# Convolutions of four blocks in one TensorE visit instead of two

## The chip, the cores and the metric

One NeuronCore of one Trainium2 chip. The metric is the device time of the whole program in microseconds (us). A run is called slow when it is over 1.5% above the fastest of its kernel. The granted TensorE clock, the share of full speed that the chip lets TensorE run at, is given where it matters.

## The reference, cut to what matters

A depthwise causal convolution of width 7 (weights by softmax, one set for each of 8 heads of 24 channels) over `x[8, 4160, 192]`, then a feed-forward layer with a three-way maximum:

```python
y = conv7(x)                                          # (33280, 192)
h = maximum(maximum(y @ w1, y @ w2), y @ w3)          # (33280, 768)
out = h @ w_out                                       # (33280, 192)
```

The kernel uses max(a, b, c) = c + max(max(a-c, 0), b-c): "layer 1" computes the two differences, "layer 2" adds them up with w_out, and a product of w3 and w_out is applied to y directly.

## The kernel before

The tokens are cut into 65 blocks of 512. TensorE does three things: layer 1 (`l1`, six groups a block, 64-row tiles, one bank `p` and one bank `q` a group), layer 2 (`st2`, six portions a block, 64-row tiles, results `po` in banks `w`), and the convolution of a later block (`conv`, 32-column tiles, two banks). A bank is here one tile of 128 x 512 fp32 in the memory that takes the results of matmuls; the kernel allocates eight (two `p`, two `q`, four `w`). An evacuation copies a result out of its bank. A conv is a product with a band matrix, per chunk of about 103 tokens and per head:

```python
def conv(t, pools=((psw, "w"), (psw, "w"))):
    G = [pool.tile([P, NBLK], FP32, tag=tag, ...) for i, (pool, tag) in enumerate(pools)]
    for (q, b, row_lo, rlen, lo, hi, cc) in chunks_of[t]:        # 5 chunks
        for i in range(2):
            for g in range(4):
                ...
                nc.tensor.matmul(G[i][32 * g:32 * g + 32, lo:hi],
                                 lhsT=x16[0:rlen, cb:cb + 32], rhs=band[0:rlen, h, cc:cc + hi - lo],
                                 start=True, stop=True, tile_position=(0, 32 * g))
...
for t in range(2, NB):                                           # cut
    l1(t, 0)
    us = convs_at.get(t, (t + 3, t + 4) if t % 2 == 0 else ())
    for n, u in enumerate(us):
        conv(u, PQ if n else ((psw, "w"), (psw, "w")))
    for u in us:
        evac(u, 0)                                               # ScalarE
    for u in us[::-1]:
        evac(u, 1, nc.vector.tensor_copy)                        # VectorE
    ...                                                          # repacks, loads, casts
    st2(t - 1, 0, NJ)
    for j in range(1, NJ):
        l1(t, j)
        st2(t - 1, j, NJ)
```

So a conv is 40 matmuls with a weight load each, and every second block TensorE makes a visit of two convs. The result of a conv goes through `ys` (four slots), six repacking DMAs and a doubling DMA before layer 1 of that block reads it.

The softmax here doesn't subtract the row's maximum and nothing guards it: scores larger than these inputs give would overflow.

## Time and profile before

| | before |
|---|---|
| time | 480.37 us (479.93 to 480.54, 3 runs) |
| span of the profiled run, granted clock | 478.4 us, 0.999 |
| TensorE busy | 97% |
| a block without a visit, with a visit of two | 6.36, 7.59 us |
| four blocks | 27.90 us |

The blocks' times are the distances between the first layer-1 matmuls of blocks that follow each other. From block 6 to 62 the pattern repeats within 0.1 us. The lines themselves stand in the prediction.

### The profile page before, as it was taken

Reading aid. Unit: us, or ns where it says so; the run is one execution under the profiler, and the core shown is the slowest. Engines: PE = TensorE matmul, PEld = TensorE weight load, DVE = VectorE, ACT = ScalarE, POOL = GpSimd, SP = SyncE. Lnnn points to the kernel's source line nnn. Section 1 sums busy time; section 2 is a strip of 40 time slices with the busy share of each in tenths; the row PEclk is TensorE's granted clock in tenths of the full one; section 3 lists DMA queues with packets and bytes.
Section 4 is the critical chain, followed back from the end, with each engine's and each line's share of the span. In section 5 each row is a group of like instructions: output and inputs, shape, how many; then the busy total and the mean of one; then the engine's idle time right before and its main releaser. Section 6 shows DMA issues by size and latency. Waiting matters only on the chain.

```text
span 478.4 us, 21790 instructions
## 1 busy us (share of the span) xinstructions
PE 466.1 (97%) x9008; PEld 390.2 (82%) x9008; DVE 368.2 (77%) x612; ACT 323.6 (68%) x602; POOL 213.6 (45%) x346
## 2 busy tenths in 40 slices
PE   7799999999999999999999999999999999999996
PEld 3377888888888888888888888888888888888995
DVE  6776877877787787778778777877877787787774
ACT  4666667667666766766676676667667666766664
POOL 3645534543453454345345434534535453454200
PEclk9999999999999999999999999999999999999999
DMA  8786766666756676675576667666666766674323
GB/s 193 170 195 188 202 186 181 173 175 172 205 155 169 170 196 171 177 201 158 158 206 169 177 171 206 166 170 187 169 155 188 206 166 168 176 182 122 98 67 100
DMA packets 68576, 81.86 MB, mean 171 GB/s; under 512 B 9422, under 2 KB 57486, under 8 KB 68478
## 3 DMA queue, kind: packets, MB, share of 16 engines
q1 hardware_dynamic: 55310, 49.51, 42.2%
q0 software_dynamic: 13008, 30.88, 20.9%
q8 instruction: 70, 1.15, 1.1%
q14 instruction: 28, 0.23, 0.1%
q10 hardware_dynamic: 160, 0.10, 0.1%
HBM read 30.31 MB, written 25.56 MB: 117 GB/s over the span
## 4 chain that ended last, share of the span: by engine, by line
PE 94%; DVE 2%; DMA 2%; ACT 1%; issue 0%; ACTq 0%; SPq 0%
PE lp L365 31%; PE po L409 30%; PE lq L365 26%; PE G L295 7%; DMA yd<-ys 1%; DMA yd<-yd 1%; DVE h L370 0%; DVE yd L330 0%; PE D L314 0%; PE idle L211 0%; ACT L225 0%; DVE line L228 0%; ACT r L369 0%; PE band_cols L232 0%; DVE wd L250 0%
## 5 line engine op out<-in xcount | busy, mean ns | idle before, releaser
L370 DVE TENSOR_TENSOR h<-r,lq 128x512 f16<-128x512 f16 x390 | 267.1, 685 | 100.8 <-ACT r L369 100.5
L369 ACT ACTIVATE r<-lp 128x512 f16<-128x512 f32 x390 | 232.9, 597 | 140.5 <-PE lp L365 92.8
L365 PE MATMUL lp<-yd,wd 64*128 64x512 f16 x1170 | 315.7, 376 | 2.2 <-DVE wd L250 1.6
L365 PE MATMUL lq<-yd,wd 64*128 64x512 f16 x1170 | 314.3, 375 | 2.7 <-DVE h L370 1.8
L409 PE MATMUL po<-wo,h 64*128 64x192 f16 x3120 | 230.7, 243 | 0.0
L409 PEld LDWEIGHTS <-h 64*128 64x128 f16 x3120 | 186.3, 94 | 25.8
L365 PEld LDWEIGHTS <-wd 64*128 64x128 f16 x2340 | 163.6, 93 | 28.2 <-issue 4.4
L435 POOL DMA_DIRECT2D out_dram<-o x63 | 49.9, 793 | 235.0 <-DVE o L419 227.1
L348 POOL DMA_DIRECT2D yd<-ys x186 | 94.0, 509 | 4.3 <-ACT ys L335 1.7
L409 PE MATMUL po<-m,yd 64*128 64x192 f16 x780 | 86.9, 243 | 0.0
L419 DVE TENSOR_TENSOR o<-a,po 128x384 f32<-128x384 f32 (+1 forms) x132 | 71.4, 542 | 0.6 <-ACT a L418 0.6
L418 ACT COPY a<-po 128x384 f32<-128x384 f32 (+1 forms) x132 | 61.7, 468 | 1.4 <-PE po L409 1.4
L149 POOL CAST x<-xf 112x960 f16<-112x960 f32 x61 | 60.6, 995 | 4.5 <-DMA xf<-in_x_dram 4.5
L409 PEld LDWEIGHTS <-yd 64*128 64x128 f16 x780 | 54.7, 94 | 8.3
L335 DVE CAST ys<-G 128x512 f16<-128x512 f32 x62 | 39.8, 683 | 0.0
L295 PEld LDWEIGHTS <-x 112*32 112x32 f16 x2440 | 29.0, 96 | 13.3 <-issue 13.2
L335 ACT CAST ys<-G 128x512 f16<-128x512 f32 x62 | 33.5, 588 | 1.8 <-PE G L295 0.4
L295 PE MATMUL G<-band,x 112*32 112x103 f16 (+1 forms) x2440 | 33.8, 209 | 0.0
L166 POOL CAST xz<-xf 112x240 f16<-112x240 f32 (+2 forms) x12 | 3.8, 360 | 7.7 <-DMA xf<-in_x_dram 7.7
L211 PE MATMUL idle<-idle 128*128 128x512 f16 x10 | 4.6, 628 | 1.2 <-DVE idle L206 1.2
L314 PEld LDWEIGHTS <-xz 112*32 112x32 f16 x180 | 3.6, 111 | 1.4 <-issue 1.4
L330 DVE COPY yd<-yd 64x512 f16<-64x512 f16 x6 | 2.7, 452 | 1.9 <-ACT yd L320 1.2
(48 smaller groups left out, 44.7 us busy)
## 6 DMA issues: line engine op xcount, KB each, us to landing
out_dram<-o POOLq DMA_DIRECT2D x63, 384.0 KB, 4.1
xf<-in_x_dram SPq DMA_DIRECT2D x57, 420.0 KB, 4.5
yd<-yd SPq DMA_DIRECT2D x62, 192.0 KB, 3.3
yd<-ys SPq DMA_DIRECT2D x62, 48.0 KB, 3.8
yd<-ys POOLq DMA_DIRECT2D x62, 48.0 KB, 3.5
xf<-in_x_dram SPq DMA_DIRECT2D x8, 252.0 KB, 3.5
yd<-ys SPq DMA_DIRECT2D x62, 32.0 KB, 3.3
yd<-ys POOLq DMA_DIRECT2D x62, 32.0 KB, 3.5
```

What stands on the lines that cost most here:

```text
L149: nc.gpsimd.tensor_copy(out=v[0:rl, q0:q1, :], in_=xf[0:rl, q0:q1, :])
L211: nc.tensor.matmul(ps[:], lhsT=idle[:, 0:P], rhs=idle[:], start=True, stop=True)
L295: nc.tensor.matmul(G[i][32 * g:32 * g + 32, lo:hi], lhsT=x16[0:rlen, cb:cb + 32], rhs=band[0:rlen, h, cc:cc + hi - lo], start=True, stop=T ...
L335: copy(out=slots[t][:, i, :], in_=convs[t][i][:])
L348: (nc.sync, nc.gpsimd)[n % 2].dma_start(out=yd[r0:r0 + rows, c, :], in_=slots[t][s0:s0 + rows, half, :])
L365: nc.tensor.matmul(ps[i][:, 0:N], lhsT=wd[row, c, P * j:P * (j + 1)], rhs=y[row, c, 0:N], start=(c == 0), stop=(c == NC - 1))
L369: nc.scalar.activation(out=r[:, 0:N], in_=ps[0][:, 0:N], func=AF.Relu)
L370: nc.vector.tensor_max(out=hs[t][:, j, 0:N], in0=r[:, 0:N], in1=ps[1][:, 0:N])
L409: nc.tensor.matmul(ps[b0, i][:, s % 2, :], lhsT=a, rhs=b, start=first, stop=last)
L418: nc.scalar.copy(out=a[:, ss, :], in_=ps[s0, 0][:, ss, :])
L419: nc.vector.tensor_add(out=outs[t][:, s0:s + 1, :], in0=a[:, ss, :], in1=ps[s0, 1][:, ss, :])
L435: qs[i].dma_start(out=bass.AP(tensor=out.tensor, offset=r * D, ap=[[D, n], [step * D, s1 - s0], [1, D]]), in_=ob[p0:p0 + n, s0:s1, :])
```

## The change

A visit of two costs 0.33 us beyond its matmuls, by the working in the prediction. TensorE goes from 64*128 tiles to 112*32 tiles and back there; that these two changes of tiling mode cost the 0.33 us ("the drains" below) was the author's estimate. The intent is to make half as many visits, of four convs each, in every fourth block. Four convs and a layer-1 group need ten banks and the kernel has eight, so the fourth conv takes the banks of the first, and the evacuations are put on ScalarE and VectorE in the order in which the banks are wanted. Loads and casts run two blocks further ahead.

```diff
+        relu, maxi = l1_open(t, 0)        # the ReLU and max of l1 are handed back, to be issued later
@@ loop @@
-    convs_at = {2: (4, 5), 3: (6,)}
+    loads_at = {2: (9,), 3: (10,), 4: (11, 12), 5: (13,)}
+    casts_at = {2: (6,), 3: (7, 8), 4: (9, 10), 5: (11, 12)}
+    convs_at = {2: (4, 5), 3: (6,), 4: (7, 8), 5: ()}
-        us = convs_at.get(t, (t + 3, t + 4) if t % 2 == 0 else ())
+        four = t > 5 and t % 4 == 2 and t + 3 < NB
+        if t > 5:
+            load_x(t + 8)                 # was t + 6; cast_x is t + 7, was t + 5
+        if four:
+            relu, maxi = l1_open(t, 0)
+            conv(t + 3, W)
+            conv(t + 4, PQ)
+            conv(t + 5, W)
+            relu()
+            evac(t + 3, 0)
+            evac(t + 3, 1, nc.vector.tensor_copy)
+            maxi()
+            conv(t + 6, W)
+            evac(t + 4, 0)
+            evac(t + 4, 1)
+            evac(t + 5, 1, nc.vector.tensor_copy)
+            evac(t + 5, 0)
+            evac(t + 6, 1, nc.vector.tensor_copy)
...                                        # evac(t + 6, 0) after the next l1; st2 one group later
+        if t > 3:
+            for u in casts_at.get(t, (t + 7,)):
+                cast_x(u)
         for u in repacks_at.get(t, (t + 3,)):
             repack(u)
```

## The prediction

> **What bounds the kernel now**
>
> The page first, its table of engines and its list of waits, to see which engine has no slack.
>
> ```profile
> PE 466.1 (97%) x9008; PEld 390.2 (82%) x9008; DVE 368.2 (77%) x612; ACT 323.6 (68%) x602; POOL 213.6 (45%) x346
> ...
> PE 94%; DVE 2%; DMA 2%; ACT 1%; issue 0%; ACTq 0%; SPq 0%
> ```
>
> TensorE (PE) is busy for 97% of the span and makes up 94% of the chain that ended last. VectorE, ScalarE and the DMA queues have slack on average. So a saving must be TensorE time, and any new TensorE wait costs its full length. The list of waits shows that TensorE hardly waits for another engine: its longest entries are 1.8, 1.6 and 1.4 us in total, all in the set-up.
>
> But busy is not useful: a matmul's end is modelled. So next the timeline of TensorE around one visit to the convolutions, and the table of stretches with borders at the first layer-1 matmul of each block.
>
> ```profile
> 200.75 0.38 PE L365 MATMUL lp<-yd,wd 64*128 64x512 f16 x1
> ...
> 201.18 0.38 PE L365 MATMUL lp<-yd,wd 64*128 64x512 f16 x1
> 201.28 0.38 PE L365 MATMUL lq<-yd,wd 64*128 64x512 f16 x1
> 201.58 1.10 PE L295 MATMUL G<-band,x 112*32 112x103 f16 x80
> 202.62 0.34 PE L409 MATMUL po<-m,yd 64*128 64x192 f16 x3
> ```
>
> ```profile
> core 0: us, PE busy (x) PEld busy (x) DVE busy (x) ACT busy (x) POOL busy (x), PEclk, DMA share, GB/s
> 200.75:208.34 7.59, 7.59 (x182) 6.02 (x178) 6.08 (x11) 5.40 (x11) 3.22 (x5) 1.00 0.58 162
> 208.34:214.70 6.36, 6.36 (x102) 5.87 (x98) 4.88 (x9) 4.32 (x9) 3.23 (x5) 1.00 0.79 213
> 214.70:222.29 7.59, 7.59 (x182) 6.02 (x178) 6.08 (x11) 5.40 (x11) 3.23 (x5) 1.00 0.53 145
> 222.29:228.65 6.36, 6.36 (x102) 5.87 (x98) 4.87 (x9) 4.32 (x9) 3.23 (x5) 1.00 0.71 186
> ```
>
> A block with a visit takes 7.59 us, one without 6.36; the pattern repeats to 0.01 us, so nothing stalls there. Six layer-1/layer-2 groups take 6 x 1.06 = 6.36. A visit of two convs (80 matmuls) therefore costs 7.59 - 6.36 = 1.23 us. The 80 start between 201.58 and about 202.47 (201.58 + 1.10 - 0.21 for the last one's length), four at a time in the four column tiles: 20 waves of about 45 ns, 0.90 us. What is left, 1.23 - 0.90 = **0.33 us, is the price of entering and leaving**. One can see it at both edges: 0.30 us from the last layer-1 start to the first conv start, 0.15 from the last conv to layer 2, where 0.1 and 0.05 are normal. The waits of the weight loads name it from another side:
>
> ```profile
> PEld L295 <- issue: 13.2, 31, 0.4
> ```
>
> 31 times, about 0.43 us each, a conv's first weight load comes late with nothing to wait for that the profile sees: it is not pulled ahead over the last layer-1 matmuls as other loads are.
>
> A check on the split: the single conv of block 6 (40 matmuls at 40.96) leads to layer 2 at 41.54, 0.58 us after its first start, against 1.04 for the pair. A conv costs about 0.46, and the rest comes once per visit.
>
> [...]
>
> [...] Layers 1 and 2 run as 64*128 tiles, the convs as 112*32, so each visit has two changes[...]. [...]
>
> **The change part by part**
>
> *Removed.* From block 6 on there are 28 visits of two convs now (at t = 6, 8, ..., 60); afterwards 14 of four (t = 6, 10, ..., 58). The matmuls are the same. Two visits cost 2 x 1.23 = 2.46; one of four, unstalled, 0.33 + 4 x 0.45 = 2.13 to 2.15. Saved 0.32 x 14 = **4.5 us**. This is the ceiling: 475.9.
>
> *Added: waits for banks inside the visit.* I lay the new order on the measured times, with zero at the first layer-1 matmul (200.75). Durations: ReLU 0.60, ScalarE evacuation 0.585, with starts 0.48 to 0.49 apart where they are queued (ReLU at 200.54, copy at 201.03); VectorE max 0.685 and evacuation 0.68, starts 0.60 apart; about 0.05 from an end to the waiter's start (a VectorE max that ended at 13.29 let TensorE go at 13.34).
>
> - TensorE: layer 1 from 0, convs t+3 at 0.83, t+4 at 1.28, t+5 at 1.74, done issuing at 2.19. Their banks are free: t+4 needs the max of the block before (ended 1.10), t+5 the add of the last output (ended 1.57), 0.15 before it is wanted.
> - ScalarE: ReLU 0.85, evacuation of t+3 at 1.49, of t+4 at 1.97 and 2.45, of t+5 at 2.93 to 3.52.
> - VectorE: t+3 at 1.49 to 2.17, max of layer 1 to 2.78, t+5 to 3.38, t+6 to 3.98.
> - Conv t+6 takes the banks of t+3, free at 2.17 + 0.05 = 2.22, where TensorE is ready at 2.19: wait 0.03. It ends issuing at 2.68.
> - Layer 1 of j=1 starts about 2.80; its q bank is free at 2.83, within the 0.1 by which q follows p anyway: 0 to 0.03.
> - Layer 2 then takes the banks of t+5. TensorE is ready at 3.46; ScalarE frees the bank at 3.52 + 0.05 = 3.57: wait **0.11**. If ScalarE's starts were 0.585 apart instead, 0.4.
> - After that ScalarE is behind by one evacuation (t+6, to about 4.7), the ReLU of j=2 comes at 4.84 as its matmuls end, and the max at 6.15 just makes layer 1 of j=4 (wanted at 6.21). VectorE needs 0.60 to 0.87 of the 1.06 us of a group and catches up.
>
> Sum of waits 0.14 per visit, 2 us in 14.
>
> *Moved.* One of eight evacuations goes from VectorE (0.68) to ScalarE (0.585): ScalarE gets 14 x 0.585 = 8 us, from 68 to 69% of the span. Beside TensorE, not on its path. Loads and casts move two blocks earlier with the same four buffers; transfers take 4.5 us against 6.97 per block, casts 1.0 us, and a cast is due a block ahead. Repacks stay one per block. No cost expected. The 0.9 us wait for a doubling at 40.2 comes before the changed part and stays.
>
> **Sum:** 480.4 - 4.5 + 2.0 = 477.9; I say **477.8 us**.
>
> **The rivals**
>
> 1. *Evacuation takes it all back.* A burst of eight evacuations, a ReLU and a max in about 3 us: 5 x 0.49 + 0.6 = 3.05 us of ScalarE, 4 x 0.6 = 2.4 of VectorE. For: the margins above are 0.03 to 0.15 us, and at 0.585 spacing the wait for layer 2 alone is 0.4, above the gain of 0.32. Against: overlap of queued starts is in the trace. It would make 480 to 482.
> 2. *The waits vanish.* If the banks come free by 3.46, only the drains count: 475.9. For: one order of queues was clearly laid out by need of banks. Against: by the measured spacing the ReLU and the four evacuations that come first on ScalarE end at 3.52.
> 3. *A lasting disturbance.* The steady loop of ReLU, max and bank has almost no slack: 0.85 + 0.60 + 0.69 + latencies against two groups (2.12); a delay could run on through several groups. 482 or more. Against: today's visit puts ScalarE and VectorE behind too, and no wait of TensorE follows.
> 4. *Transfers.* Later loads or a blocked GpSimd queue starve the convs. Against: loads get earlier, and GpSimd is at 45%.
>
> **Range and chances**
>
> Between the ceiling (475.9) and the first rival: 475.8 to 480.6, eight times in ten. A gain over 2% (below 470.8) would need 9.6 us, twice all drains that are removed: 1%. A loss over 2% needs 0.7 us per visit on top of the lost gain: 2%. Within 2%: 97%.
>
> **What would show it**
>
> Right: 17 late conv weight loads instead of 31; a cycle of four blocks takes 4 x 6.36 + 2.1 to 2.4 us (27.55 to 27.85) instead of 27.90; in the list of waits TensorE waits for ScalarE's evacuation at layer 2 about 0.1 us, 14 times; a conv run of 160 matmuls some 1.8 to 2.0 us long, with a small gap before the last 40. Wrong: four blocks at 27.9 or more with waits of 0.3 us and up at layer 2 or at the fourth conv (rival 1); layer-1 waits after the visit (rival 3); the same number of late loads with the gain absent, which would mean that the 0.33 us is not a cost per visit; conv waits for casts or loads (rival 4).

## The result, and the profile after

| | before | after |
|---|---|---|
| time | 480.15 us (478.62 to 480.54, 4 runs) | 496.31 us (492.93 to 500.36, 4 runs) |
| ratio of the fast runs | | 1.032, 95% interval 1.025 to 1.038 |
| span of the profiled run, granted clock | 478.4 us, 0.999 | 496.7 us, 0.985 |

A ratio is the mean time of one kernel's fast runs over that of the other's fast runs of the same rounds, so it is not quite the ratio of the medians. Six runs of the kernel after are on record; two of them (500.36 and 500.46 us) count as slow and are left out of the ratio. The change made the kernel 3% slower, far outside the predicted range, and its time now varies by 7 us from run to run.

The chain that ended last, from the page of the kernel after:

```profile
PE 89%; DMA 4%; issue 3%; DVE 2%; ACT 1%; SPq 0%; ACTq 0%
```

TensorE's share fell from 94 to 89%. 3% of the span, some 15 us, is now "issue": an engine stood on the chain and waited for nothing that the profile records. DMA doubled to 4%. The list of waits of the kernel after (total us, times, longest us) says which engine:

```profile
PEld L295 <- issue: 16.4, 24, 3.2
PEld L370 <- issue: 9.8, 16, 3.8
PE G L295 <- issue: 8.1, 5, 3.0
...
PE lq L370 <- DVE h L375: 4.5, 4, 3.5
...
DVE ys L335 <- DMA yd<-ys: 4.1, 1, 4.1
...
ACT ys L335 <- DMA yd<-ys: 3.3, 1, 3.3
```

Before, the conv's weight loads had 31 such gaps of at most 0.4 us, the drains. The number fell to 24, but the longest is now 3.2 us, and five conv matmuls themselves stood still, in the midst of a visit, for up to 3.0 us. The last three lines are another event, a single one. Next the stretches of the kernel after from the first layer-1 matmul of a block with a visit to that of the next block, for the blocks 10, 14, 22, 30, 42, 46, 54 and 58 (length first, then busy time and instructions of each engine, granted clock, DMA):

```profile
94.95:104.16 9.21, 8.94 (x263) 6.98 (x259) 6.81 (x12) 7.29 (x14) 3.22 (x5) 1.00 0.74 196
123.24:136.66 13.42, 10.41 (x261) 7.45 (x258) 6.87 (x12) 7.28 (x14) 3.23 (x5) 0.87 0.63 168
183.71:192.37 8.66, 8.66 (x262) 6.92 (x259) 6.79 (x13) 7.24 (x14) 3.22 (x5) 1.00 0.47 123
240.02:250.66 10.64, 8.85 (x263) 7.04 (x260) 6.90 (x12) 7.30 (x14) 3.23 (x5) 1.00 0.68 177
325.20:334.88 9.68, 8.83 (x262) 7.19 (x258) 6.79 (x12) 7.24 (x14) 3.23 (x5) 1.00 0.62 174
353.96:364.25 10.29, 8.74 (x261) 7.01 (x258) 6.88 (x12) 7.22 (x14) 3.23 (x5) 1.00 0.61 172
411.19:419.84 8.65, 8.65 (x262) 6.91 (x258) 6.78 (x12) 7.23 (x14) 3.23 (x5) 1.00 0.73 194
438.92:451.04 12.12, 10.51 (x286) 7.49 (x283) 6.88 (x13) 7.23 (x14) 2.30 (x4) 0.86 0.38 95
```

The undisturbed visits (the third and the seventh line) give a block of 8.65 us, and 8.65 + 3 x 6.36 = 27.73 for four blocks: the predicted size, 0.17 less than 27.90. But most visits are longer, by up to 4.8 us, and not at random: every fourth visit (blocks 14, 30, 46) is bad, and every fourth (22, 38, 54) is clean. TensorE's timeline in block 22 and in block 14 of the kernel after:

```profile
184.54 2.11 PE L295 MATMUL G<-band,x 112*32 112x103 f16 x160
186.59 0.39 PE L370 MATMUL lp<-yd,wd 64*128 64x512 f16 x1
```

```profile
124.07 1.96 PE L295 MATMUL G<-band,x 112*32 112x103 f16 x151
129.04 0.29 PE L295 MATMUL G<-band,x 112*32 112x103 f16 x9 [3.01 <-issue]
...
130.75 0.63 PE L370 MATMUL lp<-yd,wd 64*128 64x512 f16 x1
```

In block 22 the 160 matmuls start without a break. In block 14 TensorE stops after 151, not at the border of a conv (these lie at 40, 80 and 120), so it is not a bank that is waited for: a conv writes to both its banks within its first eight matmuls. After the gap a layer-1 matmul takes 0.63 us in place of 0.38: the granted clock is 0.50 from 129.9 to 133.3 us (0.87 in the mean of that block). In this trace gaps of 1.6 and 3.0 us (blocks 58 and 14) were followed by 3.4 us at 0.50 each, others of 1.5 and 1.8 us (blocks 46 and 30) were not: there the clock stayed at 1.00.

Where the 18.3 us of the two profiled runs went, from the blocks' times: 14 visits x 0.17 saved gives -2.4; the first visit (block 6) lost 6.4; the other 13 lost 14.7 in all against clean visits; the start and the blocks before 6 differ by -0.4.

**The theory.** TensorE ran out of instructions. The page's instruction queue has the clue:

```profile
q8 instruction: 70, 1.15, 1.1%
```

This line is the same before and after. The 70 packets have 16,384 bytes each, and TensorE has 18,016 matmuls and weight loads, 257 for each packet; in the first experiment below it has 3,584 fewer, and there are 14 packets fewer, one for each 256. So q8 brings TensorE's instructions in pieces of 256. A visit of four issues 320 instructions in 1.84 us, so a piece lasts 256 x 1.84 / 320 = 1.5 us there; in a layer-1/layer-2 group it lasts 256 / 32 x 1.06 = 8.5 us. A visit of two had 160 in 0.9 us, so there no piece lasts less than 0.9 + 96 / 32 x 1.06 = 4.1 us (an estimate from these rates). If a refill takes 3 to 5 us (an estimate; the gaps below give 2.7 to 4.7), four in a row exhaust what is fetched and two don't.

I counted TensorE's instructions in the trace up to each gap. From block 10 on, the gaps at visits begin within four instructions of number 256 n + 450 - n, for whole numbers n; the 450 is fitted. (The minus n: the trace has 65 semaphore instructions more on this queue, about one a piece.) I call these places borders, and the distance from a visit's first conv instruction to a border ahead of it the visit's **border position**. In block 14 it is 302, and 151 matmuls are 302 instructions. Borders lie 255 instructions apart in this count, so block 14 has one at 47 too, which TensorE passed without a gap. I give the border at which the visit could run dry: the one from 133 to 387 for visits of four, from 37 to 291 for visits of three.

The trace gives a size for the refill as well, if it starts when the border before is passed. In the eight gaps of the kernel after that lie at a border (0.36 us and more), 2.7 to 4.7 us went by from the passing of the border before to the end of the gap, and TensorE had used up the 255 instructions between in 1.4 to 3.3 us.

**Rivals.** The fourth conv's wait for banks or the burst of evacuations; the long stay in the other tiling mode; transfers that collide with the visits. And for the first visit, the single event above, a fault in the order of the start.

### The profile page after: what moved, and what is told of

Same layout as the page of the kernel before. It is cut to its first block, busy times and chain, and to the rows that moved or that the text cites. A ratio compares the mean times of both kernels' runs of the same rounds, so it can differ in the third digit from the quotient of the medians.

```text
span 496.7 us, 21774 instructions
## 1 busy us (share of the span) xinstructions
PE 471.7 (95%) x9008; PEld 398.3 (80%) x9008; DVE 363.4 (73%) x598; ACT 331.5 (67%) x616; POOL 213.6 (43%) x346
## 4 chain that ended last, share of the span: by engine, by line
PE 89%; DMA 4%; issue 3%; DVE 2%; ACT 1%; SPq 0%; ACTq 0%
PE po L414 28%; PE lq L370 28%; PE lp L370 26%; PE G L295 6%; DMA yd<-yd 2%; DMA yd<-ys 2%; DVE h L375 1%; ACT r L374 1%; PE D L314 1%; PE idle L211 0%; ACT L225 0%; SPq L348 0%; DVE line L228 0%; PE band_cols L232 0%; DVE wd L250 0%
## 5 line engine op out<-in xcount | busy, mean ns | idle before, releaser
L370 PE MATMUL lq<-yd,wd 64*128 64x512 f16 x1170 | 318.8, 379 | 6.5 <-DVE h L375 4.5
L370 PE MATMUL lp<-yd,wd 64*128 64x512 f16 x1170 | 320.4, 380 | 2.1 <-DVE wd L250 1.8
L414 PE MATMUL po<-wo,h 64*128 64x192 f16 x3120 | 239.2, 244 | 1.1 <-issue 1.1
L414 PEld LDWEIGHTS <-h 64*128 64x128 f16 x3120 | 194.7, 95 | 22.1 <-issue 3.1
L370 PEld LDWEIGHTS <-wd 64*128 64x128 f16 x2340 | 167.3, 94 | 35.6 <-issue 9.8
L414 PE MATMUL po<-m,yd 64*128 64x192 f16 x780 | 91.7, 245 | 0.0
L414 PEld LDWEIGHTS <-yd 64*128 64x128 f16 x780 | 59.2, 95 | 12.0 <-issue 2.6
L335 ACT CAST ys<-G 128x512 f16<-128x512 f32 x76 | 40.3, 594 | 4.8 <-DMA yd<-ys 3.3
L295 PEld LDWEIGHTS <-x 112*32 112x32 f16 x2440 | 29.2, 96 | 14.8 <-issue 14.7
L335 DVE CAST ys<-G 128x512 f16<-128x512 f32 x48 | 32.1, 687 | 11.6 <-PE G L295 6.8
L314 PE MATMUL D<-band,xz 112*32 112x103 f16 (+1 forms) x180 | 4.1, 236 | 0.0
```

The costliest lines, as they stand in the source:

```text
L295: nc.tensor.matmul(G[i][32 * g:32 * g + 32, lo:hi], lhsT=x16[0:rlen, cb:cb + 32], rhs=band[0:rlen, h, cc:cc + hi - lo], start=True, stop=T ...
L314: nc.tensor.matmul(ps[32 * g:32 * g + 32, lo:hi], lhsT=xz[t][0:rlen, q, v, 32 * s:32 * s + 32], rhs=band[0:rlen, h, cc:cc + hi - lo], star ...
L335: copy(out=slots[t][:, i, :], in_=convs[t][i][:])
L370: nc.tensor.matmul(ps[i][:, 0:N], lhsT=wd[row, c, P * j:P * (j + 1)], rhs=y[row, c, 0:N], start=(c == 0), stop=(c == NC - 1))
L414: nc.tensor.matmul(ps[b0, i][:, s % 2, :], lhsT=a, rhs=b, start=first, stop=last)
```

## The experiments

### The same visits, a fifth of the instructions

```diff
-        for (q, b, row_lo, rlen, lo, hi, cc) in chunks_of[t]: ...        # 40 matmuls of about 103 columns
+        for i in range(2):                                              # blocks 9 to 64: 8 of 512
+            for g in range(4):
+                nc.tensor.matmul(G[i][32*g:32*g+32, :], lhsT=x16[0:rlen, cb:cb+32],
+                                 rhs=flat_band[0:rlen, s0:s0+512], start=True, stop=True, ...)
```

The results are wrong; banks, waits, evacuations and transfers stay.

> The changed kernel with the convs of blocks 9 to 64 done as 8 matmuls of 512 columns each in place of 40 of about 103 (wrong results on purpose; same columns streamed per column tile[...], same banks, waits, evacuations and transfers, a fifth of the instructions: 64 instead of 320 in a visit). Theory A (TensorE runs out of fetched instructions: a visit's 320 instructions pass in 1.8 us, faster than a refill of 256 arrives): no idle time of TensorE put down to issue in or after any visit, 13 of the 14 cycles of four blocks at 27.6 to 27.8 us; only the first cycle stays near 34. About 484 us in all, 482 to 487. Theory B (the fourth conv's wait for banks, or four convs' evacuations, or a long stay in the other tiling mode, is what stalls TensorE): the gaps stay and it takes 492 to 500 as the changed kernel does.

Measured: 479.06 us (477.88 to 480.88, 4 runs), ratio to the kernel before 0.998 (0.993 to 1.002), against 1.032 for the change. Blocks 14 and 22, the stretches of this run's trace:

```profile
120.32:128.83 8.51, 8.51 (x133) 6.12 (x131) 6.80 (x12) 7.16 (x14) 3.23 (x5) 1.00 0.64 180
175.51:184.02 8.51, 8.51 (x134) 6.11 (x131) 6.89 (x12) 7.15 (x14) 3.23 (x5) 1.00 0.65 190
```

In block 14 the visit's 32 matmuls take 1.85 us from the first start to layer 1; the 160 in block 22 of the kernel after take 2.05. All visits but the first now take 8.51 to 8.56 us, and no TensorE matmul waits for issue. Twelve of the 14 cycles are 27.59 us, one 27.64, and the first 32.88. The total is 5 us below what I had expected, which I can explain only in part. The cycles are 0.14 us shorter than clean ones, and the trace shows where: ScalarE's evacuations start 0.14 us sooner in the visit (the first at 1.35 us after 1.49), and layer 2, which waits for the last of them, starts at 3.45 us instead of 3.59. With the same banks, evacuations, transfers and stay in the tiling mode, the gaps go when the instructions go. As a check of the queue, it has 56 packets here:

```profile
q8 instruction: 56, 0.92, 0.8%
```

56 convs x 64 instructions fewer = 3,584 = 14 packets of 256.

### Moving the border, and nothing else

```diff
     keep_warm(6)
+    for _ in range(34):                                                  # 68 instructions
+        nc.tensor.matmul(ps_shift[:, 0:32], lhsT=idle[:, 0:P], rhs=idle[:, 0:32], start=True, stop=True)
```

> The changed kernel with 34 tiny matmuls (68 instructions) more before the loop, in TensorE's idle time at the start. In the changed kernel's trace the idle gaps put down to issue begin at instruction 256 n + 450 - n of TensorE to within 3. Theory A: the border between fetched pieces moves 68 instructions earlier relative to every visit, so the gaps move to other visits: the visits at blocks 14, 30 and 46 (excess 4.8, 2.0, 1.6 us before) go down to under 0.5; those at blocks 22, 38 and 54 (0 before) get about 1, 1 and 1.5 us; 10, 26 and 42 get 1.5 us or more (0.6, 0.8, 1.0 before); 18, 34 and 50 stay under 0.3. Theory B: a count of instructions before the loop moves nothing; the same visits stall.

Measured: 494.17 us (one run, state unknown). Loss of each cycle of four blocks against 27.73 us, with the border position of its visit:

| visit at block | after: position, loss (us) | shifted: position, loss (us) |
|---|---|---|
| 10 | 370, 0.6 | 302, 1.9 |
| 14 | 302, 4.8 | 234, 1.1 |
| 18 | 234, 0.2 | 166, 0 |
| 22 | 166, 0 | 353, 1.0 |
| 26 | 353, 0.8 | 285, 2.5 |
| 30 | 285, 2.0 | 217, 0.3 |
| 34 | 217, 0 | 149, 0 |
| 38 | 149, 0 | 336, 0.9 |
| 42 | 336, 1.0 | 268, 4.2 |
| 46 | 268, 1.6 | 200, 0 |
| 50 | 200, 0.1 | 387, 0.3 |
| 54 | 387, 0 | 319, 1.9 |
| 58 | 319, 3.5 | 251, 0.3 |

Matmuls issued before the loop moved the stalls to other visits, to the ones named in advance: 22, 38 and 54 now stall, 46 no longer does and 30 hardly. One miss: block 14 was to lose under 0.5 and lost 1.1, at position 234, which the kernel after had at block 18 with a loss of 0.2. The loss at a position varies from run to run, but in both runs all positions from 268 to 370 lost 0.6 us or more and those from 149 to 217 at most 0.3; 234, 251 and 387 lie between. The blocks 22 and 46 of this run:

```profile
177.08:186.75 9.67, 8.85 (x261) 6.78 (x258) 6.80 (x13) 7.28 (x14) 3.23 (x5) 1.00 0.65 174
...
352.41:361.06 8.65, 8.65 (x261) 6.89 (x258) 6.78 (x12) 7.24 (x14) 3.23 (x5) 1.00 0.56 160
```

### The first visit: one queue

```diff
         if t > 3: ... cast_x(...)
+        # at t == 5, repack(8) stands before the casts of blocks 11 and 12
```

> The changed kernel with the repack of block 8 issued before the casts of blocks 11 and 12 at t = 5. The first visit lost 6.4 us because an evacuation waited for the repack DMA of block 8 to have read the slot (4.1 us in VectorE's queue, 3.3 in ScalarE's), and that DMA stood behind a cast in GpSimd's queue that waited for a load. Theory (that queue is the cause of the first visit's loss, apart from the rest): the first cycle goes from 34.2 to 27.7 to 28.5 us, no wait of ScalarE or VectorE for the repack is left there, and the whole takes some 6 us less than the changed kernel: 487 to 492. Rival (the first visit stalls for the same reason as the others): no change there.

Measured: 495.34 us (491.74 to 498.54), ratio 1.033. The first cycle took 31.1 us in place of 34.2 and the waits were still there. They read, in this run:

```profile
DVE ys L335 <- DMA yd<-ys: 3.9, 1, 3.9
ACT ys L335 <- DMA yd<-ys: 3.0, 1, 3.0
```

So this order is not shown to have done anything. The kernel after ran 6.8 us at a granted clock of 0.50 in this cycle, which is worth up to 3.4 us, and this run none (0.998 in the mean of the run); and the shifted run above, with the old order and also the full clock there (0.994 in the mean of the run), took 30.6 us with waits of 3.4 and 2.5 us. SyncE's queue showed the next suspect: the doubling of block 7 went out only at 61.0 us, and the repack of block 8 stood behind it.

### The first visit: three queues

```diff
-        if t in (4, 5): load all of loads_at[t]
+        if t in (4, 5): load the first of loads_at[t]      # load_x(12) comes after repack(7)
+        # at t == 4 and 5 the repack stands before the casts
```

> The changed kernel with blocks t = 4 and 5 ordered anew: each repack before the casts in GpSimd's queue, and the load of block 12 issued after the repack of block 7. In the run that moved one repack alone, the doubling of block 7 was still issued only at 61.0 us because the repack of block 7 came late: behind a cast that waited for a load in GpSimd's queue, and behind the loads of blocks 11 and 12 in the transfers; it holds the later repack of block 8 in SyncE's queue. Theory: with these out of the way no evacuation waits for a repack, and the first cycle of four blocks takes 27.7 to 28.4 us in place of 34.2 and 31.1; the other cycles stall as before (14 visits, the same positions), so 485 to 491 us in all. If the first cycle stays above 30, the cause is another.

Measured: 495.35 us (one run, state unknown), above the expected 485 to 491, because three visits (blocks 30, 46 and 58) lost 3.8 to 4.3 us each in this run, whose mean granted clock was 0.985. The first cycle took 29.43 us, less than before but not the 28.4 that I had expected at most, and an evacuation still waited:

```profile
DVE ys L335 <- DMA yd<-ys: 2.2, 1, 2.2
ACT ys L335 <- DMA yd<-ys: 1.3, 1, 1.3
```

So the order of these queues is likely a part of it, some 1.2 us against the 30.6 us of the shifted run, from one run each; most is left. What the wait is for is plain from its line: the fourth conv of a visit at t writes the slot of block t + 2, whose repack is issued only in block t - 1; the kernel before never came closer than t - 3. The runs of three blocks below, which reuse slots no later than those of t + 1, show no such wait, and there block 6 took 8.17 us, near the 8.08 of the others. What else delays the repack of block 8 at the start I did not settle.

### Three blocks in a visit

Three convs and a layer-1 group fill the kernel's eight banks, so no conv waits for a bank; 240 instructions.

```diff
-        four = t > 5 and t % 4 == 2 and t + 3 < NB
+        four = t > 5 and t % 3 == 0 and t + 3 < NB
-            conv(t + 6, W)      # and its evacuations
```

> Visits of three blocks every third block (240 instructions, 1.37 us of array time); three convs and the layer-1 tiles fill the eight banks exactly, so no conv waits for a bank. A visit without stalls should cost 0.33 + 3 x 0.455 = 1.70 us, a cycle of three blocks 3 x 6.36 + 1.70 = 20.78. Theory A: where a piece's border falls near the visit, [...] so about half of the 18 visits lose 0 to 1.5 us, put down to issue, after the visit; 478 to 483 us. Theory B by the bank wait: no bank wait, no gap, all 18 cycles at 20.8 us, 477.5 us.

Measured: 485.16 us (482.62 to 488.09), ratio 1.010 (1.004 to 1.016), somewhat more than I had expected of the theory and far from the 477.5 of the rival. Twelve of the 18 visits of three give blocks of 8.04 to 8.17 us, near what was worked out (6.36 + 1.70). The six others lost 0.8 to 1.9 us, 7.5 in all, without any conv having waited for a bank. (The expectations below count seven: the seventh is the last visit, of two blocks, which had a gap of 0.5, but not at a border. From border to the end of the gap it took 3.2 to 4.5 us in the six.) Five positions repeat, 183, 132, 81, 285 and 234, and only the visits at 285 and 234 stalled. The blocks 12 (81), 15 (285) and 18 (234):

```profile
102.84:110.93 8.09, 8.09 (x222) 7.05 (x218) 6.76 (x12) 5.92 (x12) 3.23 (x5) 1.00 0.71 204
123.65:133.47 9.82, 8.30 (x221) 6.92 (x218) 6.75 (x12) 5.88 (x12) 3.23 (x5) 1.00 0.74 194
146.19:155.38 9.19, 8.27 (x222) 6.57 (x218) 6.84 (x12) 5.89 (x12) 3.22 (x5) 1.00 0.57 162
```

The stall need not fall within the visit. In block 15 TensorE ran 23 more layer matmuls after the convs and then stopped, at instruction 286:

```profile
124.52 1.56 PE L295 MATMUL G<-band,x 112*32 112x103 f16 x120
...
127.33 0.29 PE L414 MATMUL po<-m,yd 64*128 64x192 f16 x2
129.14 0.25 PE L414 MATMUL po<-m,yd 64*128 64x192 f16 x1 [1.51 <-issue]
```

A reader who looked at this gap alone would blame layer 2. By the theory, the convs had used up what was fetched 1.3 us earlier.

### Putting the visits where the border is not

The positions can be computed from the program, and a visit may also stand at the fourth layer-1 group of a block, 96 instructions later, where again no `po` bank is in use. These two runs, which also have the early order of three queues from above, move two of five visits each: once the bad ones, once two good ones.

```diff
+    def place(t): return 3 if (t - 6) // 3 % 5 in (3, 4) else 0      # second run: in (1, 2)
-        l1(t, 0), convs, evacuations; then groups 1 to 5
+        the convs and evacuations stand at group place(t)
```

> Visits of three blocks, with the same early order, and with two visits in five (those whose first matmul stood 285 and 234 instructions before the border at which the fetched instructions end; the only two of the five positions that stalled in the run of three blocks) moved from the first layer-1 group of a block to the fourth, 96 instructions later. Theory A: all 18 visits then stand at positions 81, 132, 138, 183 and 189, none stalls, each block with a visit takes 8.03 to 8.10 us, and the whole 477 to 479 us, a ratio of 0.995 to 0.998 to the kernel before. Theory B (stalls come from banks, evacuations or transfers near the visits and not from the count of instructions): the number of stalls stays about 7 in 18, 482 to 487 us.

> As the run before it, but with the other two positions moved by the same 96 instructions: 132 goes to 36 (291 to the next border) and 81 to -15 (240). Same instructions, same number of moved visits. Theory A: four of five positions now stall, 14 of 18 visits, by 0.5 to 2 us each as the seven of the run of three blocks did (1.1 on average): about 493 us, 487 to 498. Theory B: the same time as the run before it.

Measured, bad ones moved: 478.63 us (476.39 to 479.74, 6 runs) against 480.83 (478.12 to 483.74, 11 runs) for the kernel before, ratio 0.995 (0.991 to 0.999). The blocks 15 and 18, which had taken 9.82 and 9.19:

```profile
123.97:132.06 8.09, 8.09 (x221) 7.05 (x218) 6.76 (x12) 5.89 (x12) 3.23 (x5) 1.00 0.55 149
144.78:152.87 8.09, 8.09 (x222) 7.11 (x218) 6.77 (x12) 5.90 (x12) 3.23 (x5) 1.00 0.54 151
```

17 of 18 visits were clean within 0.15 us; block 21 (position 183) lost 0.7, which I had not expected. Its gap stands at the border too: 4.6 us went by from the border before, and TensorE had used up the instructions in 3.9. So a good position makes a stall rare, not impossible.

Good ones moved: 489.79 us (488.30 to 498.64), ratio 1.018 (1.014 to 1.023), "unclear" by the 2% rule. The two kernels have the same instructions and as many moved visits, and differ by 11 us. The profiled execution was a slow one, so I read from it only which visits lost over 0.35 us: 14 of them, at blocks 9, 12, 15, 18, 24, 27, 30, 33, 39, 42, 45, 48, 54 and 57, exactly the 14 that had been put on bad positions. The other four visits of three took 8.05 to 8.29 us.

The same with the change itself, visits at blocks 14, 18, 30, 46 and 58 moved:

> The change itself (four blocks in every fourth block) with the early order and with the visits at blocks 14, 18, 30, 46 and 58 moved to the fourth layer-1 group. Theory A: the visits left at a bad position are those at 10, 26 and 42 (370, 353, 336), which lose 0.3 to 1.1 us each as they did; all others take 8.65 us or little more; 479 to 484 us in all, against 496 for the change. Theory B: no better than the change with the early order alone, 485 or more.

Measured: 480.70 us (479.70 to 482.14), ratio 1.001 (0.997 to 1.005). Losses left: 0.4, 1.0 and 0.9 at blocks 10, 26 and 42, as named in advance, 0.4 at the moved block 14, and 2.1 in the first cycle. Moving five visits and the order of the start took the change from 496 to 481 us.

## Why the prediction was wrong

- *What bounds the kernel, and the price of a visit (0.33 us).* Right. The clean cycle of four blocks is 27.73 us, in the range named (27.55 to 27.85) and 0.01 off the middle estimate of 27.90 - 0.18.
- *The waits for banks inside the visit (0.14 us each).* Right in size and in place: 2.46 - (8.65 - 6.36) = 0.17 was saved of 0.32, so 0.15 went back. In the run of three blocks, which has no such wait, the visit cost 1.72 where 1.70 had been worked out. The sign named for it, an entry in the list of waits, did not come, but the timeline of block 22 of the kernel after (first layer-1 matmul at 183.71) has it, ScalarE's evacuations first and then the start of layer 2:

```profile
185.20 2.05 ACT L335 CAST ys<-G 128x512 f16<-128x512 f32 x4
187.30 0.32 PE L414 MATMUL po<-m,yd 64*128 64x192 f16 x3
```

  ScalarE's four evacuations end at 3.54 us and layer 2 starts at 3.59, where the prediction had 3.52 and 3.57.
- *"Removed: ... The matmuls are the same."* This is the step that failed. The same matmuls come in bursts of 320 instructions in place of 160, and I priced a visit by array time alone, with the supply of instructions taken as free. In its place the runs showed a cost that grows with the burst, as TensorE stands still at the borders of the fetched pieces: next to nothing at 160 instructions, 7.5 us in 18 visits at 240, and 14.7 us in 13 visits at 320, up to 3.4 of it because the granted clock was 0.50 for 3.4 us after two of the gaps. None of my four rivals had it, though the line of the instruction queue stood on the page of the kernel before.
- *"Moved: ... No cost expected."* Failed as well, and less: 6.4 us at the first visit, up to 3.4 of it by the 6.8 us at a granted clock of 0.50. The fourth conv reuses a slot whose repack is one block old, and at the start that repack was late. Rival 4, against which I had said that loads get earlier, was near it, but why the repack was late is not shown: the two runs with the early order of three queues still lost 1.7 and 2.1 us there.
- *What would show it.* The signs that I had named would have told right from wrong: the cycles, and the waits of the convs. "17 late weight loads" was right: of the 24 in the list 17 are the drains of 0.42 us, five are stalls, and two are short ones of 0.2.
- *The chances.* 2% for slower by over 2% was too sure: I had reasoned over banks, engines and transfers and left no room for a resource that I had not listed.

The mechanism of the stalls is shown by three kinds of run: fewer instructions end them (a ratio of 0.998 in place of 1.032), 68 instructions ahead of the loop move them (block 22 loses 1.0 us in place of 0, block 46 0 in place of 1.6), 96 instructions' distance for a visit makes or ends them (489.79 or 478.63 us). Why a refill takes as long as it does is only seen in part: in block 14 of the kernel after, the packet of q8 started 1.85 us after the visit did, just as TensorE ran dry, took 1.75 us, and TensorE went on 1.4 us after it had ended. Why it did not start earlier, and how much of this is due to the other transfers, I have not tested.

## What to carry to other kernels

Here TensorE was held up by its supply of instructions: 32 in 1.06 us and bursts of 160 in 0.9 us left next to no gaps, bursts of 320 in 1.84 us cost 14.7 us in 13 visits. So before short matmuls are put together, count the instructions in the burst, and compare the time in which one fetched piece (256 here) is used up (1.5 us in a visit of four, at least 4.1 with visits of two) with the time of a refill (estimated at 2.7 to 4.7 us from the gaps here). Gaps of 0.4 to 3.0 us put down to issue, in the midst of a run of equal instructions or shortly after one, that began a multiple of 255 apart in the instruction count were its mark; moving the count by a few dummy instructions tests it in one run. If the burst can't have fewer instructions, its place in the program can be chosen: with it, visits of three blocks came to 0.995 of the kernel before, 2.2 us, near the 3.0 us that nine visits fewer at 0.33 us were worth.
